# Moving the tiles of a matmul-bound kernel to start addresses that are multiples of 512 bytes

## Chip, cores and metric

The kernel runs on one core of one Trainium2 chip. The metric is the device time of one execution in microseconds (us), as the median of several runs. Durations of single instructions come from one profiled execution.

## What is computed

Three stages on 1536 tokens (2 batches of 768) with 512 features, all in float32:

```python
# 1. chunked attention, 8 heads of 64; a chunk of 32 queries sees 16 tokens left,
#    8 right, and 8 memory slots
scores = scale * np.matmul(q_c, k_full.transpose(0, 1, 3, 2))
a = np.exp(scores - np.max(scores, axis=-1, keepdims=True))
a = a / (np.sum(a, axis=-1, keepdims=True) + 1e-09)
out[:, :, c_start:c_end] = np.matmul(a, v_full)
# 2. a feed-forward layer 512 -> 2048 -> 512 with a rational function
h = x @ w_in;  h2 = h * h;  h3 = h2 * h
P = a[0] + a[1] * h + a[2] * h2 + a[3] * h3
Q = 1.0 + np.abs(b[0]) * np.abs(h) + np.abs(b[1]) * h2
x = (P / (Q + 1e-6)) @ w_out
# 3. four experts 512 -> 1024 -> 512, mixed with given shares
p = domain_probs / (domain_probs.sum(-1, keepdims=True) + 1e-09)
for e in range(4):
    h = np.maximum(x @ w1[e], 0.0)
    out += p[:, e:e + 1] * (h @ w2[e])
```

## The kernel before

**The large products.** Stages 2 and 3 multiply with TensorE. Each float32 operand is split into a high and a low half, both of type float32r, and each product is made of three matmuls (high with high, low with high, high with low; `PAIRS`). One such matmul has 128 x 128 stationary weights, a moving operand of 128 x 512 elements (2048 bytes in each partition) and one PSUM bank as its output. Each has a weight load of its own (512 bytes in each partition). There are 3366 of them:

- Stage 2 runs 48 steps (3 blocks of 512 tokens by 16 slices of 128 hidden features), each with 12 matmuls of `first_ops` (line 568: moving tile `x`, stationary tile `w`) and 12 of `second_ops` and `mm` (line 680: moving tile `g`, stationary tile `w`).
- Stage 3 runs 16 chunks of 256 hidden features. Chunk 0 has 72 matmuls at line 568 and 72 at line 927. Each of the chunks 1 to 15 has 42 matmuls at line 794 (seven products in Strassen's manner for two of the three blocks, stationary from `w`), 24 at line 568 (the third block) and 72 in `second` (line 927: moving tile `w`, stationary tile `g` or `gb`). Of the seven products at line 794, four move a tile `x`, and three move a sum of activations that lies in a tile `w`.

**The other engines.** VectorE (DVE), ScalarE (ACT) and GpSimd (POOL) split the weights and the activations, evaluate the rational function and read the PSUM banks out. All DMAs are issued by the SP queue.

**The order.** A planner (`Plan`) with costs and due times makes one list of operations; each engine gets its instructions in the order of that list. When the list is worked off, `make` allocates each tile at the operation that takes it first, and then the operation is recorded.

**Where tiles lie.** All tiles come from one pool. A tag gets its buffers side by side when it is taken for the first time, and the tags follow each other in that order, with no gap. In each partition 16,384 bytes of scratch and four constants of 32 bytes come first, then `ident` (512 bytes), `mask` (256), `cf` (64) and `pr` (192), which end at byte 17,536. Behind them lie, in the order of the list:

| tag | buffers x bytes | first byte | modulo 512 |
|---|---|---|---|
| `w` (weights, sums, attention's operands) | 10 x 8192 | 17,536 | 128 |
| `tm` | 2 x 2048 | 99,456 | 128 |
| `st` (row maxima and sums of attention) | 6 x 32 | 103,552 | 128 to 288 |
| `stg` (loaded weights) | 3 x 4096 | 103,744 | 320 |
| `x` (moving activations) | 12 x 4096 | 116,032 | 320 |
| `y`, `tu`, `ts` | 2, 2, 3 x 2048 | 165,184 | 320 |
| `g` | 4 x 4096 | 179,520 | 320 |
| `p` | 3 x 8192 | 195,904 | 320 |
| `gb` | 2 x 4096 | 220,480 | 320 |

Within these tiles every matmul at lines 568, 680, 794 and 927 begins at a multiple of 512 bytes, so that its operands begin at 128 modulo 512 if they lie in `w`, and at 320 modulo 512 if they lie in `x`, `g` or `gb`. `w` ends below byte 99,456; `x`, `g` and `gb` lie above byte 116,032.

The loop that allocates and records, lines 1102 to 1106:

```python
        for o in listed:
            for b in o.takes:
                make(b)
            o.fn()
            turn_over(fill.get(o, 0))
```

Of the kernel before, what the change touches and what calls it, by code (L numbers as in the profile page):

```python
# [11 lines left out]
F32 = mybir.dt.float32  # L12
# [33 lines left out]
AHEAD = 12  # L46
FU = 11
RU = 12
FGAP = 0.5
LAG = 3  # L50
GS = 4, 4, 4, 4
# [45 lines left out]
class Plan:  # L97
# [7 lines left out]
    def add(self, ways, fn, after=(), uses=(), takes=(), key=None, lock=False):  # L105
        op = Op(len(self.ops), ways, fn, key)
        op.lock = lock
        self.ops.append(op)
        for a in after:
            if a is not None:  # L110
                op.after.append(a)
                a.next.append(op)
        op.takes = list(takes)
        op.bufs = list(takes) + list(uses)
        for b in op.bufs:
            b.users.append(op)
        return op
# [133 lines left out]
def emit(ctx: ExitStack, tc: tile.TileContext, qk, v0, kv, q8, w64, w32, coef, prob, out):  # L251
# [8 lines left out]
    def sb(shape, dt, tag, name=None):  # L260
        return pool.tile(shape, dt, tag=tag, bufs=BUFS.get(tag, 1), name=name or tag)

    def bank(tag):
        return Buf(tag, [128, 512], F32)

    def make(b):
        p = psum if b.tag in ("acc", "h", "att") else pool
        b.ap = p.tile(b.shape, b.dt, tag=b.tag, bufs=BUFS[b.tag], name=b.tag)
# [22 lines left out]
    def turn_over(n):  # L291
        for _ in range(n):
            PE.matmul(idle.ap, zeros.ap[:, :128], zeros.ap, start=True, stop=True)
# [98 lines left out]
    class Unit:  # L392
# [5 lines left out]
        def psum_buf(self):  # L398
            if self.u >= RU:
                return bank("att")  # L400
            Unit.turn = (getattr(Unit, "turn", -1) + 1) % 6
            return bank((["att"] * 2 + ["acc"] * 4)[Unit.turn])
# [655 lines left out]
    o = add([("SP", 0.1)], load_probs, [steps[nA - 1].firsts[0]])  # L1058
# [30 lines left out]
    listed = plan.run()  # L1089
# [4 lines left out]
    for a, b in zip(pe, pe[1:]):  # L1094
        if a.n == last:
            break
        n = int((b.start - a.end - FGAP) / MM)
        if n > 0:
            fill[a] = min(n, 16)
    with tc.manual_schedule():  # L1100
        ACT.preload_act_table_set("natural_log_exp_and_others")
        for o in listed:
            for b in o.takes:
                make(b)
            o.fn()
            turn_over(fill.get(o, 0))

# [76 lines left out]
```

## Time and profile before

| | |
|---|---|
| median of 3 runs | 856.23 us (856.16 to 857.15) |
| the profiled execution | 855.45 us |
| its span, first to last instruction | 853.7 us |
| TensorE matmul busy | 835.5 us (98%) |
| DVE busy | 624.7 us (73%) |
| POOL busy | 380.6 us (45%) |
| ACT busy | 357.8 us (42%) |
| granted TensorE clock | 0.999 of full speed |

The profile lists instructions by line, engine and tile, each with its start. A matmul's own duration in it (some 390 ns) is the way of one matmul through a pipelined array: several overlap. What a matmul costs in a row of them is the distance from its start to the next one's start, so it is read from the starts of groups, or from the chain of work that ended last, which lists back-to-back stretches with their number of matmuls. The profile has no addresses; they are those of the table above.

### The profile page before, as it was taken

The page shows a single profiled execution, that of the slowest core. Times are in us where ns is not written, and L with a number is a line of the kernel's source. Part 1 is how long each engine was busy: PE and PEld are TensorE (multiplying, and loading weights), DVE is VectorE, ACT ScalarE, POOL GpSimd, SP SyncE. Part 2 cuts the span into 40 slices and gives each one's busy share as a digit, 9 for nine tenths or more (in the row PEclk, how much of TensorE's full clock was granted, in tenths as well). Part 3 has the DMA queues.
Part 4 walks back from the last instruction along what each step waited for, and adds up shares of the span by engine and source line. Part 5 has one row for each costly group of instructions (what it writes and reads, how often), then busy time and mean ns, then how long its engine had stood idle before and what let it go on. Part 6 is the DMA issues. An engine that isn't in the chain of part 4 may idle for free.

```text
span 853.7 us, 11342 instructions
## 1 busy us (share of the span) xinstructions
PE 835.5 (98%) x4214; PEld 665.2 (78%) x4218; DVE 624.7 (73%) x929; ACT 357.8 (42%) x783; POOL 380.6 (45%) x350
## 2 busy tenths in 40 slices
PE   7889999999999999999999999999999999999998
PEld 4667788778788887788888888888888888888886
DVE  6987799999996779775775775775765765765754
ACT  6798877756757665231231231231230230230210
POOL 4797776877678788440330330330330330330300
PEclk9999999999999999999999999999999999999999
DMA  9975122212212001010110110110110100100003
GB/s 350 362 263 194 51 74 74 90 60 74 74 49 52 1 0 50 1 51 0 50 40 10 50 38 12 49 32 18 50 30 20 50 28 22 50 25 1 1 1 147
DMA packets 21911, 55.41 MB, mean 65 GB/s; under 512 B 3936, under 2 KB 3936, under 8 KB 21856
## 3 DMA queue, kind: packets, MB, share of 16 engines
q1 hardware_dynamic: 21856, 54.69, 18.6%
q8 instruction: 33, 0.54, 0.3%
q14 instruction: 22, 0.18, 0.1%
HBM read 51.54 MB, written 3.15 MB: 64 GB/s over the span
## 4 chain that ended last, share of the span: by engine, by line
PE 66%; DVE 21%; ACT 4%; DMA 3%; POOL 3%; issue 2%; SPq 0%; DVEq 0%; ACTq 0%; POOLq 0%
PE acc L927 31%; PE att L568 11%; PE h L794 10%; PE att L794 7%; DVE ts L649 4%; PE h L568 3%; PE acc L680 3%; DVE tm L637 2%; DVE tm L641 2%; DVE p L699 2%; DVE y L357 2%; DVE y L363 1%; DVE y L351 1%; DVE att L649 1%; DMA w<-kv 1%
## 5 line engine op out<-in xcount | busy, mean ns | idle before, releaser
L325 POOL TENSOR_TENSOR w<-stg,w 128x512 fp32r<-128x512 f32 x64 | 97.0, 1525 | 325.4 <-ACT w L280 325.4
L944 DVE SCALAR_TENSOR_TENSOR p<-acc,pr,p 128x512 f32<-128x512 f32 x180 | 135.1, 751 | 107.1 <-PE acc L927 106.8
L927 PE MATMUL acc<-w,g 128*128 128x512 f32 x768 | 182.0, 397 | 0.5 <-DVE p L942 0.5
L927 PEld LDWEIGHTS acc<-w,g 128*128 128x128 f32 x768 | 144.9, 189 | 35.1 <-DVE p L942 1.4
L568 PE MATMUL att<-x,w 128*128 128x512 f32 x624 | 151.9, 395 | 1.5 <-DVE ts L649 1.5
L680 PE MATMUL acc<-g,w 128*128 128x512 f32 x576 | 146.3, 399 | 2.1 <-DVE p L699 1.6
L568 PEld LDWEIGHTS att<-x,w 128*128 128x128 f32 x624 | 116.9, 187 | 30.5 <-DVE ts L649 1.9
L680 PEld LDWEIGHTS acc<-g,w 128*128 128x128 f32 x576 | 106.9, 188 | 29.9 <-DVE p L699 3.0
L280 ACT ACTIVATE ts<-h 128x512 f32<-128x512 f32 x15 | 9.0, 599 | 246.0 <-PE h L794 246.0
L568 PE MATMUL h<-x,w 128*128 128x512 f32 x384 | 98.2, 400 | 0.5 <-DVE ts L649 0.3
L927 PE MATMUL acc<-w,gb 128*128 128x512 f32 x384 | 92.0, 397 | 0.0
L927 PEld LDWEIGHTS acc<-w,gb 128*128 128x128 f32 x384 | 72.6, 189 | 16.9
L568 PEld LDWEIGHTS h<-x,w 128*128 128x128 f32 x384 | 70.8, 188 | 17.7 <-POOL w L325 0.6
L325 POOL TENSOR_TENSOR g<-ts,g 128x512 fp32r<-128x512 f32 x48 | 66.7, 1391 | 26.8 <-ACT g L280 26.3
L668 POOL TENSOR_TENSOR ts<-ts,tu 128x512 f32<-128x512 f32 x48 | 63.3, 1320 | 12.9 <-ACT ts L657 9.6
L325 POOL TENSOR_TENSOR w<-y,w 128x512 fp32r<-128x512 f32 x36 | 49.9, 1387 | 8.3 <-ACT w L280 8.0
L280 ACT ACTIVATE g<-ts 128x512 fp32r<-128x512 f32 x48 | 30.3, 631 | 39.9 <-DVE ts L649 39.8
L794 PE MATMUL h<-x,w 128*128 128x512 f32 x180 | 46.8, 395 | 0.0
L794 PE MATMUL att<-x,w 128*128 128x512 f32 x180 | 46.8, 395 | 0.0
L794 PE MATMUL h<-w 128*128 128x512 f32 x180 | 46.0, 391 | 0.0
L794 PEld LDWEIGHTS h<-x,w 128*128 128x128 f32 x180 | 33.8, 188 | 8.2
L794 PEld LDWEIGHTS att<-x,w 128*128 128x128 f32 x180 | 33.8, 188 | 8.0
(122 smaller groups left out, 1167.8 us busy)
## 6 DMA issues: line engine op xcount, KB each, us to landing
stg<-w SPq DMA_DIRECT2D x64, 512.0 KB, 3.7
w<-kv SPq DMA_DIRECT2D x32, 256.0 KB, 5.9
w<-q SPq DMA_DIRECT2D x16, 256.0 KB, 5.8
w<-qk SPq DMA_DIRECT2D x8, 400.0 KB, 5.8
out<-p SPq DMA_DIRECT2D x12, 256.0 KB, 2.0
w<-v SPq DMA_DIRECT2D x8, 256.0 KB, 7.4
pr<-prob SPq DMA_DIRECT2D x1, 24.0 KB, 3.9
cf<-coef SPq DMA_DIRECT2D x1, 3.0 KB, 7.1
```

Source lines behind the costliest of these rows:

```text
L280: return lambda o, i: ACT.activation(o, i, AF.Copy)
L325: engines[op.eng].tensor_tensor(out=dst[:, 1], in0=src, in1=dst[:, 0].bitcast(F32), op=ALU.subtract)
L357: DVE.scalar_tensor_tensor(out=y.ap, in0=words(1), scalar=-(1 << 30), in1=y.ap, op0=ALU.bitwise_and, op1=ALU.bitwise_or,)
L568: PE.matmul(s.h.ap, wt[w].ap[:, 0, a, k * 128 : (k + 1) * 128], xs[k].ap[:, b], start=(k == 0 and n == 0), stop=(k == KT - 1 and n == 2),)
L637: [("DVE", 0.6)], lambda: DVE.tensor_tensor(out=m.ap, in0=m.ap, in1=h.ap, op=ALU.mult), [li], [h, m]
L641: lambda: DVE.scalar_tensor_tensor(out=m.ap, in0=m.ap, scalar=A1, in1=h.ap, op0=ALU.add, op1=ALU.mult),
L649: lambda: DVE.scalar_tensor_tensor(out=out.ap, in0=in0.ap, scalar=scalar, in1=in1.ap, op0=op0, op1=op1),
L668: lambda: POOL.tensor_tensor(out=s.ap, in0=s.ap, in1=u.ap, op=ALU.mult), [ln], [s, u],
L680: PE.matmul(ps, wt[f].ap[:, 1, a, d * 128 : (d + 1) * 128], g.ap[:, b], start=start, stop=stop)
L794: PE.matmul(ps.ap, left(a, k), right(b, k), start=k == 0 and n == 0, stop=k == 1 and n == 2,)
L927: PE.matmul(ps.ap, gs[j][0].ap[:, a, d * 128 : d * 128 + 128], wt[f].ap[:, 1, b], start=j == 0 and n == 0, stop=j == 1 and n == 2,)
L944: DVE.scalar_tensor_tensor(out=y, in0=ps.ap, scalar=p, in1=y, op0=ALU.mult, op1=ALU.add)
```

## The change

Ahead of the loop the buffers of tag `st` are now allocated, and behind them a tile `pad` of 192 bytes that nothing reads or writes. The loop leaves out the one buffer that has been made already.

```diff
+PAD = 192 // 4
 ...
     with tc.manual_schedule():
         ACT.preload_act_table_set("natural_log_exp_and_others")
+
+        make(next(b for o in listed for b in o.takes if b.tag == "st"))
+        sb([128, PAD], F32, "pad")
         for o in listed:
             for b in o.takes:
-                make(b)
+                if b.ap is None:
+                    make(b)
             o.fn()
             turn_over(fill.get(o, 0))
```

So `st` starts at byte 17,536 and `pad` at 17,728, and `w` starts at 17,920, which is 35 x 512. `w` and `tm` move up by 384 bytes, every later tag by 192 bytes, and all tags from `w` on start at 0 modulo 512. `gb` ends at byte 228,864. Every engine has the same instructions in the same order, with the same waits; only addresses in SBUF differ. No instruction is added, removed or moved.

## Rows read from the trace of the kernel before

**Rows 1.** Page, busy time by engine; then windows: busy us and instructions of each engine.

```profile
PE 835.5 (98%) x4214; PEld 665.2 (78%) x4218; DVE 624.7 (73%) x929; ACT 357.8 (42%) x783; POOL 380.6 (45%) x350
...
core 0: us, PE busy (x) PEld busy (x) DVE busy (x) ACT busy (x) POOL busy (x), PEclk, DMA share, GB/s
110.00:250.00 140.00, 138.11 (x586) 109.59 (x586) 132.91 (x186) 96.24 (x163) 105.73 (x81) 1.00 0.21 72
250.00:320.00 70.00, 70.00 (x302) 56.43 (x300) 50.09 (x74) 45.60 (x78) 53.50 (x46) 1.00 0.07 16
362.00:835.00 473.00, 473.00 (x2035) 382.78 (x2034) 307.68 (x424) 107.61 (x190) 112.66 (x85) 1.00 0.09 28
```

**Rows 2.** Waits of PE in the whole span: engine, line, releaser, us, times, longest.

```profile
PE acc L680 <- DVE p L699: 1.6, 2, 0.9
PE att L568 <- DVE ts L649: 1.5, 1, 1.5
```

**Rows 3.** Chain that ended last, 496 to 529 us: start us, us, what.

```profile
496.56 1.40 PE h L794 x6
497.96 1.40 PE att L794 x6
499.36 1.38 PE h L794 x6
500.74 1.38 PE att L794 x6
502.12 1.36 PE h L794 x6
503.48 1.40 PE att L794 x6
504.88 1.40 PE h L794 x6
506.28 5.60 PE att L568 x24
511.88 16.80 PE acc L927 x72
528.68 1.40 PE h L794 x6
```

**Rows 4.** Timeline of PE, 499 to 506 us: which tiles those products read.

```profile
499.19 1.54 PE L794 MATMUL h<-w 128*128 128x512 f32 x6
501.96 1.52 PE L794 MATMUL h<-w 128*128 128x512 f32 x6
503.32 1.56 PE L794 MATMUL att<-x,w 128*128 128x512 f32 x6
506.12 5.76 PE L568 MATMUL att<-x,w 128*128 128x512 f32 x24
```

**Rows 5.** Timeline of PE near 36 us, and line 293: bfloat16 matmuls on zeros.

```profile
36.57 1.24 PE L293 MATMUL acc<-tm 128*128 128x512 bf16 x5 [0.16 <-issue]
...
L293 PE MATMUL acc<-tm x16: 379/384/634, 1.2 to 48.0; 128*128 128x512 bf16 x16
```

**Rows 6.** Waits of DVE, 110 to 250 us.

```profile
DVE y L351 <- POOL w L325: 2.4, 2, 1.2
DVE ts L649 <- ACT h L672: 1.6, 3, 0.9
```

**Rows 7.** Chain that ended last, 100 to 345 us (stage 2): pieces on PE and one on DVE.

```profile
105.55 4.67 PE acc L680 x20
113.72 2.81 PE h L568 x12
120.71 1.25 DVE y L363
```

**Rows 8.** Groups by line and shape: VectorE reading tile tm (128) and tile ts (320).

```profile
L637 DVE TENSOR_TENSOR tm<-tm,h 128x512 f32<-128x512 f32 x29 | 19.7, 678 | 1.9 <-ACT tm L634 1.8
L649 DVE SCALAR_TENSOR_TENSOR ts<-ts,h 128x512 f32<-128x512 f32 x29 | 19.7, 678 | 0.2
```

## The prediction

> **What bounds the kernel now.** I read the busy times first, then the waits of PE, then the chain of work that ended last. PE is busy for 835.5 of 853.7 us [rows 1], and the two longest sums of waits that the list of PE's waits has are 1.6 and 1.5 us [rows 2]. So PE works almost throughout, and the question is what one matmul costs there. The granted clock is 1.00 in every stretch [rows 1], that is 2.4 GHz, at which 512 columns take 512 / 2.4 = 213.3 ns. The chain shows whole stretches in which each matmul follows the one before: 24 at line 568 take 5.60 us and 72 at line 927 take 16.80 us, both 233.3 ns each [rows 3]; stage 2 has the same, 20 at line 680 in 4.67 us and 12 at line 568 in 2.81 us, 233.5 and 234 ns [rows 7]. Each costs 20 ns more than its columns.
>
> Not every matmul does. The reader should look at the seven pieces of line 794 in one chunk: four of 1.40 us, two of 1.38 us and one of 1.36 us, for six matmuls each [rows 3]. The shape, the weight loads, the number of matmuls per PSUM bank and the halves used are the same in all seven. The timeline tells what differs: the short ones read only `w` ("h<-w"), the long ones read `x` and `w` [rows 4]. By the table of addresses both operands of the short ones begin at 128 modulo 512; in the long ones the moving operand begins at 320 and the stationary one at 128. At line 927 it is the other way round, moving `w` at 128 and stationary `g` or `gb` at 320, and it costs 233.3 ns as well. So in the trace of the kernel before there are two classes: both operands at 128, 226.7 ns (1.36 / 6) to 230 ns (1.38 / 6); one of them at 320, 233.3 ns. The difference is up to 6.7 ns, and the change puts all of them into one class.
>
> There is a third row, of another type: five bfloat16 matmuls on a zero tile at 128 modulo 512 are busy for 1.24 us together, and one of them lasts 0.384 us by the median [rows 5], so four distances make 0.86 us, 215 ns each, 1.7 ns over 512 columns. It is the nearest row for a matmul without the extra time.
>
> **The change part by part.** *Added work:* none. `pad` is never read or written, no engine gets an instruction, and `make` runs when the program is built, not on the chip. *Bytes:* all transfers and all operands are as large as before. *PSUM:* no address moves.
>
> *VectorE, ScalarE, GpSimd.* Their operands move too. The profile has VectorE reading the tile `tm` (at 128) and the tile `ts` (at 320), each with one PSUM operand, at 678 ns in both [rows 8]. I take their prices as unchanged. For what lies at neither of the two offsets there is no row; the bounds are nothing on either side, because stage 3 would hide some per cent on an engine that is busy for 307.68 of 473 us [rows 1], and stage 2 would not. If VectorE changed by 1% there, it would be some 1.3 of 132.91 us either way, and I leave that to the range.
>
> *The matmuls.* The new offsets are 0 and 0 everywhere. Like 128 and 128 they are equal, and like 128, 0 is a multiple of 128 bytes, which 320 is not. No row has an fp32r operand at 0, so the price is bounded. From above it is 233.3 + 6.7 = 240 ns (one more step of the size seen, see the rivals); from below it is the 215 ns of the bfloat16 row. I take the row nearest in type, shape and kind of address, the pieces that read only `w`: 1.38 us per six for the first two products of a chunk and 1.36 us from then on, as now.
>
> Sum against the profiled execution (855.45 us), stretch by stretch:
>
> 1. Chunks 1 to 15. Now the seven products take 4 x 1.40 + 2 x 1.38 + 1.36 = 9.72 us; then 2 x 1.38 + 5 x 1.36 = 9.56 us. Line 568 goes from 5.60 to 24 x 0.2267 = 5.44 us, line 927 from 16.80 to 16.32 us. That is 0.16 + 0.16 + 0.48 = 0.80 us a chunk of 32.12 us (496.56 to 528.68 us [rows 3]), and 12.0 us in 15. Nothing else is late there: DVE is busy for 307.68 and POOL for 112.66 of 473 us [rows 1], and the chain runs on PE alone [rows 3].
> 2. Chunk 0: 144 matmuls x 6.7 ns = 0.96 us at most. PE waits there for 1.5 us for DVE in one place [rows 2]; I take 0.7 us.
> 3. The last part of stage 2, 250 to 320 us: PE is busy for all 70.00 us with 302 matmuls, DVE for 50.09 and POOL for 53.50 [rows 1]. 302 x 6.7 ns = 2.0 us, all of it.
> 4. The middle of stage 2, 110 to 250 us: 586 matmuls, 3.9 us at most. But DVE is busy for 132.91 of these 140 us, with 2.4 us of waits for POOL and 1.6 us for ACT in its row of waits [rows 1, 6], and the chain passes through DVE [rows 7]. A faster PE here mostly waits for DVE's rational function and its conversions. I take a third, 1.3 us.
> 5. The rest of stage 2 (48 x 24 = 1152 in all, less 302 and 586: some 260 matmuls, in groups between the attention's small ones and at the change of stages): 1.7 us at most. The first 26 us have no large product and stay. I take 0.5 us.
>
> The sum is 12.0 + 0.7 + 2.0 + 1.3 + 0.5 = 16.5 us, so the profiled execution would be 838.95 us. The median of the runs is 0.78 us above the profiled execution; from the median it is 856.2 - 16.5 = 839.7 us. If all of 1 to 5 came, it would be 12.0 + 0.96 + 2.0 + 3.9 + 1.7 = 20.6 us, 835.6 us. If every matmul stayed at 230 ns, as in the first two products, half of it would come, some 8 us: 848 us. These are this forecast's own ends.
>
> **The rivals.** *The extra time goes altogether.* The 13.3 ns that are left at 128 and 128 (226.7 - 213.3) may themselves come from the start. For it: 128 bytes are 32 columns of 4 bytes, which take 13.3 ns, and from 320 to the next multiple of 256 it is 192 bytes, 48 columns, 20.0 ns. That is just the extra time of the two classes, as if the way to the next multiple of 256 were paid. Against it: the same 20 ns come where only the weights lie at 320, so that it would have to be the worse of two ways rather than their sum, and the bfloat16 row at 128 pays hardly any of it. At 215 ns a chunk saves 120 x 18.3 + 18 x 13.9 ns = 2.45 us (228.9 ns is the mean of the three pieces on `w`), 36.7 us in 15; chunk 0 saves 2.0, stretch 3 some 4.5 (POOL's 53.50 us would then stand against 65), stretches 4 and 5 some 3 as DVE holds them. That is 46 us: 810 us.
>
> *Nothing changes.* What separates the classes may be where tiles lie rather than at which offset they start: the short ones have both operands below byte 99,456, the others have one above 116,032, and the change keeps that. The trace can't tell the two, as every tile above starts at 320. Also for it: the same two tiles ("h<-w") cost 230 or 226.7 ns in one chunk, at one offset, so something else than the offset has a hand in it. Then the time stays 856.2 us. Against it: nothing in the trace suggests that one reading of 512 columns is slower by its place. The Trainium skill (TensorE: Matmul & The Clock Gate, section "Wait — 56ns, not 53.3ns?") speaks for this rival: it gives the distance of warm matmuls by the columns alone, 215.7 ns at 512, with no term for an address, and its page SBUF — State Buffer (section "Operand start alignment") calls the start address a matter of legality, not speed. By that rule the sum would be nothing; the bfloat16 row agrees with it, and the two classes of float32r rows, both above 215.7 ns, do not.
>
> *Slower.* While a matmul streams, the weights of the next are read. If the two readings disturb each other when both begin at the start of the same 512-byte stretch, the step of 6.7 ns would be added to 233.3 instead of being taken away: 240 ns. The path is PE alone, so it would count in full: 3096 x 6.7 ns + 270 x 11 ns = 24 us, 880 us. It decides as soon as a matmul at 0 and 0 costs more than 233.3 ns. Against it: the fastest rows today are those with equal offsets.
>
> **How the numbers follow.** The forecast, 839.7 us, has 0.47; all of the extra time gone, 810 us, 0.25; no change, 856.2 us, 0.20; slower, 880 us, 0.08. A range that leaves out at most 2 in 10 can do without the slower case alone, as 0.08 + 0.20 or 0.08 + 0.25 is already too much; it runs from the floor case to no change with a little for the spread of the runs, 809 to 858 us. Faster and slower are told apart at 0.2% (1.7 us), about what a measurement of this kernel can tell. From the four cases: faster 0.47 + 0.25 = 0.72, same 0.19, slower 0.09, with 0.01 of the third case beyond the bound.
>
> **What would show it.** In the chain of the changed kernel, line 927's 72 matmuls should take 16.3 us, line 568's 24 should take 5.44 us, and the seven products at line 794 should take the same time each whether they read `x` or not. 16.80 us again would mean that the place and not the offset makes the classes; 15.5 us would be the rival in which all of it goes. In stage 2 PE's waits for DVE at lines 649 and 699 should grow between 110 and 250 us, and hardly elsewhere. VectorE's 678 ns should stay. The prediction is wrong if matmuls cost the same as before, or if PE gains in stage 3 and loses it to waits that are not there now.

## The result and the profile after

The changed kernel takes 843.36 us as the median (843.05 to 844.18) beside 856.19 us for the kernel before (855.07 to 857.15): ratio 0.9851, 95% interval 0.9837 to 0.9865. It is 12.8 us faster; 16.5 us were forecast. The profiled execution took 843.32 us.

The chain of work that ended last, in the same chunk as [rows 3] (start us, us, what; lines are one higher than before):

```profile
493.71 1.36 PE h L795 x6
495.07 1.36 PE att L795 x6
496.43 1.36 PE h L795 x6
497.79 1.36 PE att L795 x6
499.15 1.36 PE h L795 x6
500.51 1.36 PE att L795 x6
501.87 1.36 PE h L795 x6
503.23 5.44 PE att L569 x24
508.67 16.32 PE acc L928 x72
524.99 1.36 PE h L795 x6
```

All seven products take 1.36 us, and so do the others in proportion: 5.44 / 24 and 16.32 / 72 are 226.7 ns. The class of 233.3 ns is gone. A chunk takes 524.99 - 493.71 = 31.28 us instead of 32.12.

Up to there next to nothing has come of it. The same piece, the third block's products in chunk 1, begins at the same time in both executions, as their chains show, of the kernel before:

```profile
378.12 5.60 PE att L568 x24
```

and of the changed kernel:

```profile
378.11 5.44 PE att L569 x24
```

Counted from the first large matmul of stage 2, which starts at 26.79 us in the one and at 27.32 us in the other, it comes 0.5 us earlier in the changed kernel.

Stage 2 says how. The windows (busy us and instructions of PE, PEld, DVE, ACT, POOL), of the kernel before from 110 to 345 us:

```profile
110.00:345.00 235.00, 231.60 (x986) 184.49 (x986) 207.58 (x292) 154.94 (x262) 178.27 (x141) 1.00 0.16 52
```

and of the changed kernel, with the two parts that answer to [rows 1] and the waits of PE from 110 to 345 us (engine, line, releaser: us, times, longest):

```profile
110.00:345.00 235.00, 228.96 (x986) 185.17 (x984) 206.72 (x293) 154.74 (x261) 178.98 (x141) 0.99 0.16 52
...
110.00:250.00 140.00, 136.08 (x581) 109.51 (x580) 132.59 (x187) 95.90 (x161) 105.94 (x81) 0.99 0.21 72
250.00:320.00 70.00, 70.00 (x310) 57.87 (x310) 49.55 (x73) 45.97 (x78) 53.48 (x47) 1.00 0.06 16
...
PE acc L681 <- DVE p L700: 3.0, 3, 2.1
PE att L569 <- DVE ts L650: 1.7, 1, 1.7
```

PE starts 986 matmuls in these 235 us in both kernels. It is busy for 2.64 us less and waits longer for DVE: 3.0 us for the read-outs at line 700 instead of the 1.6 us of [rows 2]. The chain at the longest of these waits runs on DVE alone, of the changed kernel:

```profile
228.43 0.75 DVE ts L650
229.17 0.67 DVE h L650
229.84 2.38 DVE p L700 x4
```

In the kernel before the same four read-outs are a piece of the same length:

```profile
229.27 2.38 DVE p L699 x4
```

DVE reaches them no earlier with a faster PE: here 0.57 us later, in an execution whose large matmuls began 0.53 us later. They stand behind DVE's own queue, and PE's next matmuls at line 681 need the banks that they free.

The two parts by themselves, 581 matmuls instead of 586 up to 250 us and 310 instead of 302 from there on, mislead, because the granted clock fell in this execution behind that wait. A window of it, and the 12 matmuls that follow the wait:

```profile
232.00:234.00 2.00, 2.00 (x5) 1.43 (x5) 2.00 (x5) 1.15 (x3) 0.56 (x2) 0.50 0.03 8
...
230.58 5.34 PE L681 MATMUL acc<-g,w 128*128 128x512 f32 x12 [2.07 <-DVE p L700]
```

The clock of 0.50 is the level of 1.2 GHz; from 236 us it is 1.00 again. The 12 matmuls take 235.76 - 230.58 = 5.18 us. One kernel of the next section (everything at 128) has the same instructions and matmuls as fast, and its clock stayed at 1.00 here:

```profile
110.00:250.00 140.00, 135.88 (x587) 109.47 (x586) 132.01 (x186) 95.89 (x162) 106.55 (x81) 1.00 0.22 72
250.00:320.00 70.00, 69.31 (x303) 56.30 (x301) 50.06 (x74) 45.63 (x78) 53.54 (x47) 1.00 0.06 16
...
229.26 2.38 DVE p L700 x4
...
229.99 4.03 PE L681 MATMUL acc<-g,w 128*128 128x512 f32 x12 [2.09 <-DVE p L700]
```

Its large matmuls begin at 26.69 us, and DVE's read-outs start within 0.01 us of where they start in the kernel before. The 12 matmuls take 3.88 us (to 233.87) behind a wait as long, and the two parts have 587 and 303 matmuls, one more in each than before. So DVE's pace leaves PE next to nothing in either part; the 310 of the changed kernel only made up for what the low clock had cost (581 + 310 = 891 matmuls, here 587 + 303 = 890). The piece in chunk 1 begins at 377.63 us there, 0.4 us earlier by the count from the first large matmul.

### The profile page after: what moved, and what is told of

The parts are those of the page before. It is cut to its first block, busy times and chain, and to the rows that moved or that the text cites. A ratio compares the mean times of both kernels' runs of the same rounds, so it can differ in the third digit from the quotient of the medians.

```text
span 841.5 us, 11342 instructions
## 1 busy us (share of the span) xinstructions
PE 819.9 (97%) x4214; PEld 664.9 (79%) x4218; DVE 623.6 (74%) x929; ACT 356.5 (42%) x783; POOL 381.1 (45%) x350
## 4 chain that ended last, share of the span: by engine, by line
PE 65%; DVE 21%; ACT 5%; POOL 4%; issue 2%; DMA 2%; SPq 0%; DVEq 0%; ACTq 0%; POOLq 0%
PE acc L928 30%; PE att L569 10%; PE h L795 10%; PE att L795 7%; DVE ts L650 5%; PE h L569 3%; PE acc L681 3%; DVE tm L638 2%; DVE tm L642 2%; DVE p L700 2%; DVE y L358 2%; DVE y L352 1%; DVE att L650 1%; DVE y L364 1%; DMA w<-kv 1%
## 5 line engine op out<-in xcount | busy, mean ns | idle before, releaser
L928 PE MATMUL acc<-w,g 128*128 128x512 f32 x768 | 177.5, 390 | 0.7 <-DVE p L943 0.6
L569 PE MATMUL att<-x,w 128*128 128x512 f32 x624 | 147.8, 390 | 1.7 <-DVE ts L650 1.7
L569 PE MATMUL h<-x,w 128*128 128x512 f32 x384 | 96.5, 396 | 1.0 <-DVE ts L650 0.8
L928 PE MATMUL acc<-w,gb 128*128 128x512 f32 x384 | 89.6, 389 | 0.0
L669 POOL TENSOR_TENSOR ts<-ts,tu 128x512 f32<-128x512 f32 x48 | 63.8, 1329 | 12.8 <-ACT ts L658 10.9
L795 PE MATMUL h<-x,w 128*128 128x512 f32 x180 | 45.7, 389 | 0.0
L795 PE MATMUL att<-x,w 128*128 128x512 f32 x180 | 45.7, 389 | 0.0
```

What stands on the lines that cost most here:

```text
L569: PE.matmul(s.h.ap, wt[w].ap[:, 0, a, k * 128 : (k + 1) * 128], xs[k].ap[:, b], start=(k == 0 and n == 0), stop=(k == KT - 1 and n == 2),)
L669: lambda: POOL.tensor_tensor(out=s.ap, in0=s.ap, in1=u.ap, op=ALU.mult), [ln], [s, u],
L795: PE.matmul(ps.ap, left(a, k), right(b, k), start=k == 0 and n == 0, stop=k == 1 and n == 2,)
L928: PE.matmul(ps.ap, gs[j][0].ap[:, a, d * 128 : d * 128 + 128], wt[f].ap[:, 1, b], start=j == 0 and n == 0, stop=j == 1 and n == 2,)
```

## Which property of the addresses counts

The change made the starts multiples of 512 bytes, and with that also multiples of 128, and equal to each other. The forecast named the last two together. Six kernels take them apart. In all of them the instructions are the same, and each tag lies within a few hundred bytes of where the changed kernel has it, or the kernel before.

**Everything at 320.** The changed kernel without its rest of 192 bytes:

```diff
         make(next(b for o in listed for b in o.takes if b.tag == "st"))
-        sb([128, PAD], F32, "pad")
```

> The small buffers are moved ahead, but the 192 bytes are left out, so that every tile from w on begins at 320 modulo 512: both operands of each large product begin at equal offsets, and neither is a multiple of 128 bytes. Theory of equal offsets: 226.7 ns a matmul everywhere, a chunk takes 31.28 us as after the change, and the time is that of the changed kernel, 843 us. Theory of multiples of 128 bytes: both operands are off, so 233.3 ns or more everywhere, a chunk takes at least 32.2 us (the three products on w get slower too), and the time is 857 us or above. Theory of place: as after the change, 843 us.

Measured: 843.5 us, ratio 0.9854 (0.9840 to 0.9869). The chain:

```profile
496.58 1.36 PE att L795 x6
504.74 5.44 PE att L569 x24
510.18 16.32 PE acc L928 x72
```

No large operand begins at a multiple of 512 here, nor of 128, and a matmul costs 226.7 ns all the same. The rest of 192 bytes does nothing; moving `st` ahead is the whole effect. Before, its six buffers of 32 bytes stood between `tm` and `stg` and put 192 bytes between the offset of `w` and that of `x`, `g` and `gb`. The half of my reason on multiples of 128 falls. So does the rival of place: `x`, `g` and `gb` lie at the very bytes of the kernel before, and `w` 192 bytes higher.

**Everything at 128.**

```diff
-PAD = 192 // 4
+PAD = 320 // 4
```

> 320 bytes instead of 192, so that every tile from w on begins at 128 modulo 512. Equal offsets and multiples of 128 bytes both say 226.7 ns everywhere and 843 us. If only multiples of 512 count, line 928 takes more than 16.32 us for 72 matmuls: up to 230 ns each (16.56 us), as the products on w did before the change, a chunk up to 31.7 us, and 849 us.

Measured: 843.37 us, ratio 0.9848 (0.9834 to 0.9863), with 1.36, 5.44 and 16.32 us in the chain. The same 128 and 128 had cost 230 ns in two of the three products on `w` before [rows 3]. So those 230 ns were no price of the offset 128, but an after-effect of the slower matmuls ahead of them.

**Different starts, all multiples of 128.** Rests between the tags: `w` at 0, `x` at 128, `g` at 256, `gb` at 384.

```diff
+PADS = {'x': 128, 'g': 128, 'gb': 128}
 ...
             for b in o.takes:
+                if b.tag in PADS:
+                    sb([128, PADS.pop(b.tag) // 4], F32, "pad_" + b.tag)
```

> The changed kernel with more rests between the tags: w stays at 0 modulo 512, x begins at 128, g at 256, gb at 384. All are multiples of 128 bytes, and the two operands of a product begin at different offsets except for the three products on w. Theory of equal offsets: 233.3 ns at lines 569, 681, 928 and for the products that read x, 226.7 ns for the three on w, 856 us. Theory of multiples of 128 bytes: 226.7 ns everywhere, 843 us. Theory of multiples of 512: above 226.7 ns wherever x, g or gb is read, and not the same for 128, 256 and 384.

Measured: 850.84 us, ratio 0.9935 (0.9920 to 0.9950), between both forecasts. The timeline of PE (start us, busy us) shows a mixture, in stage 2 and in stage 3:

```profile
265.90 2.90 PE L682 MATMUL acc<-g,w 128*128 128x512 f32 x12
268.63 2.95 PE L570 MATMUL att<-x,w 128*128 128x512 f32 x12
271.42 2.90 PE L682 MATMUL acc<-g,w 128*128 128x512 f32 x12
...
510.31 11.06 PE L929 MATMUL acc<-w,g 128*128 128x512 f32 x48
521.21 5.75 PE L929 MATMUL acc<-w,gb 128*128 128x512 f32 x24
526.80 1.56 PE L796 MATMUL h<-x,w 128*128 128x512 f32 x6
```

From start to start: `g` at 256 moving past `w` at 0 takes 2.73 / 12 = 227.5 ns, `w` moving past `g` at 256 takes 10.90 / 48 = 227.1 ns; but `x` at 128 takes 2.79 / 12 = 232.5 ns and `gb` at 384 takes 5.59 / 24 = 232.9 ns. A difference of 256 bytes is as good as none; one of 128 or 384 is not. None of the three theories had said that.

**Smaller differences.** The same edit with 32 bytes three times: `x` at 32, `g` at 64, `gb` at 96.

> As the mixed kernel, but with smaller rests: w at 0 modulo 512, x at 32, g at 64, gb at 96. One run shows the moving operand off by 32 (lines 569 and 795) and by 64 (line 681), and the stationary one off by 64 and 96 (line 928). Theory of multiples of 128 bytes: 233.3 ns at 64 in either role, as at 320 before, and at least that at 32 and 96, so 856 us or above. Equal offsets say the same of this run. If 64-byte starts are enough when the offset of the other is 0, 226.7 ns at 64.

Measured: 856.11 us, ratio 1.0001 (0.9992 to 1.0011): with differences of 32 to 96 bytes the whole gain is gone, though `w` begins at a multiple of 512. The timeline:

```profile
266.61 2.91 PE L682 MATMUL acc<-g,w 128*128 128x512 f32 x12
269.36 2.96 PE L570 MATMUL att<-x,w 128*128 128x512 f32 x12
272.15 2.91 PE L682 MATMUL acc<-g,w 128*128 128x512 f32 x12
...
480.38 11.36 PE L929 MATMUL acc<-w,g 128*128 128x512 f32 x48
491.58 5.77 PE L929 MATMUL acc<-w,gb 128*128 128x512 f32 x24
497.19 1.56 PE L796 MATMUL h<-x,w 128*128 128x512 f32 x6
```

`g` at 64 costs 11.20 / 48 = 233.3 ns as the stationary operand, but 2.75 / 12 = 229.2 ns as the moving one; `x` at 32 costs 2.79 / 12 = 232.5 ns and `gb` at 96 costs 5.61 / 24 = 233.8 ns.

**The rule tried on the kernel before.** If only the difference modulo 256 counts, 64 bytes more behind `st`, where it stood, must do: `w` stays at 128, and the others go to 384.

```diff
+    rest = [64 // 4]
 ...
             for b in o.takes:
                 make(b)
+                if b.tag == "st" and rest:
+                    sb([128, rest.pop()], F32, "pad")
```

> The kernel before, with one edit: a rest of 64 bytes behind st, where st stands. w and tm stay at 128 modulo 512; x, g and gb go from 320 to 384, so that the two operands of every large product differ by 256 bytes, or not at all. Theory that only the difference modulo 256 counts: 226.7 ns everywhere, a chunk 31.28 us, 843 us. Theory that the operands have to begin at equal places modulo 512 or at multiples of 512: 233 ns or about that wherever x, g or gb is read, 856 us.

Measured: 843.76 us, ratio 0.9852 (0.9837 to 0.9867). The chain:

```profile
502.58 5.44 PE att L568 x24
508.02 16.32 PE acc L927 x72
```

Every product of stages 2 and 3 then has operands that differ by 256 bytes or not at all, in either role, and all cost 226.7 ns. No operand of a large product begins at a multiple of 256.

**Other differences.** `w` at 0, `x` at 64, `g` at 192, `gb` at 224 (one execution).

> The changed kernel with w at 0 modulo 512, x at 64, g at 192, gb at 224: differences that are no multiple of 256 in both roles. Theory of the difference modulo 256: between 229 and 234 ns at lines 570, 682 and 929, 226.7 to 228 ns for the three products on w, 850 to 856 us. It also tells whether the 229 ns that line 682 showed with g at 64 belong to that difference: then x at 64 gives 229 ns too, at lines 570 and 796, and 853 us; or to that line, then 233 ns and 856 us.

Measured: 851.78 us. The timeline:

```profile
263.26 2.91 PE L570 MATMUL h<-x,w 128*128 128x512 f32 x12
266.01 2.95 PE L682 MATMUL acc<-g,w 128*128 128x512 f32 x12
268.80 2.91 PE L570 MATMUL att<-x,w 128*128 128x512 f32 x12
...
480.24 11.16 PE L929 MATMUL acc<-w,g 128*128 128x512 f32 x48
491.24 5.75 PE L929 MATMUL acc<-w,gb 128*128 128x512 f32 x24
496.83 1.55 PE L796 MATMUL h<-x,w 128*128 128x512 f32 x6
```

`x` at 64 takes 2.75 / 12 = 229.2 ns, so that price belongs to the difference and not to line 682; `g` at 192 takes 2.79 / 12 = 232.5 ns moving and 11.00 / 48 = 229.2 ns stationary, `gb` at 224 takes 5.59 / 24 = 232.9 ns. So a difference that is no multiple of 256 costs 229 to 234 ns. Where the moving operand lies 64 bytes above the other modulo 256, these two kernels show 229.2 ns in each of the three cases; but line 927 of the kernel before (128 and 320) is the same difference, and it takes 233.3 ns. What sets the price among the unequal ones stays open, and so does whether a matmul is slowed by its own weight load or by the next one's: neighbours in these rows have the same starts.

## Where stage 2's share went

Theory: DVE sets the pace of stage 2 at its read-outs and at its end, and a faster PE only waits there. Rival: the matmuls of stage 2 gain nothing, or something else holds its length. To tell them apart, DVE gets less to do, with the old addresses and with the new, and the gain from the addresses is compared.

**Without the third conversion of each stage-2 weight.** The edit is the same in both kernels; the last three mantissa bits of those weights are left out.

```diff
-            o = add([("DVE", 0.6)], conv3, [o], [r, y], lock=True)
+            o = add([("DVE", 0.6)], lambda: None, [o], [r, y], lock=True)
```

> The kernel before (old addresses) without the third conversion of each stage-2 weight (line 363 there, 32 instructions, 28.3 us of DVE in all, most of it in stage 2): the last three mantissa bits of those weights are left out, nothing else. It is the base for the next run. If DVE sets the pace of stage 2, stage 3 begins earlier than at 362 us by some us; if PE does, by nearly nothing.

> The changed kernel (all tiles at 0 modulo 512) without the same conversion. Theory that DVE took back what PE gained in stage 2: with DVE relieved, stage 2 now gains from the addresses, so that stage 3 begins 3 to 6 us earlier than in the run with the old addresses and the same conversion left out, and the whole is 15.5 to 18.5 us faster than that run, against 12.9 us with the conversion. Rival, that large products of stage 2 gain nothing from the addresses themselves or that another wait (ACT, POOL) holds stage 2: stage 3 begins at the same time in both, and the whole differs by 12 to 13 us.

Measured: 851.30 us with the old addresses and 838.54 us with the new ones. The difference is 12.8 us, as with the full work, and the piece of chunk 1 begins at 374.01 and 374.00 us. The large matmuls began 1.2 us later with the new addresses (28.60 instead of 27.37 us; the granted clock was 0.87 instead of 0.93 in the first 26 us), so that stage 2 itself may have kept 1.2 us. The 3 to 6 us of the theory did not come: its expectation failed. The waits of PE with the new addresses, from 110 to 345 us:

```profile
PE att L569 <- DVE ts L650: 1.7, 1, 1.7
PE acc L681 <- DVE p L700: 1.5, 2, 0.8
```

Old addresses leave one wait of 0.4 us in this list. So PE still waits for DVE, now longest near 327 us. The last weight conversion begins at 240 us, so the relief does not reach the place where DVE is late. Whether that is the reason was tried with a relief that reaches to the end.

**Less in every step.** In addition to the conversion one of the multiplications of the rational function is left out in all 48 steps, which changes the output.

```diff
-                [("DVE", 0.6)], lambda: DVE.tensor_tensor(out=m.ap, in0=m.ap, in1=h.ap, op=ALU.mult), [li], [h, m]
+                [("DVE", 0.6)], lambda: None, [li], [h, m]
```

> The kernel before (old addresses) without the third weight conversion (last three mantissa bits of the stage-2 weights) and without one of the multiplications of the rational function (line 637: m times h, 48 instructions of 0.68 us), so that the output of stage 2 is another one; some 58 us less on DVE. It is the base of the next run. If DVE holds stage 2, its end comes earlier than in the run without the conversion alone, which began chunk 1 some 4 us earlier than the kernel before.

> The changed kernel with the same two things left out. Theory that DVE takes back in stage 2 what PE gains: with DVE relieved through all 48 steps and up to their end, stage 2 keeps 3 to 6 us of its gain, and the run is 16 to 19 us faster than the one with the old addresses. Rival, that something else holds stage 2's length (start of the run, DMA, ACT, POOL): the difference stays at 12 to 13 us, as with the full work (12.9) and without the conversion (12.8).

Measured: 849.18 us with the old addresses, 830.80 us with the new: 18.4 us apart. The windows, old addresses and then new:

```profile
110.00:345.00 235.00, 234.88 (x1007) 189.12 (x1007) 177.07 (x243) 159.33 (x269) 182.90 (x146) 1.00 0.16 52
```

```profile
110.00:345.00 235.00, 234.08 (x1030) 192.89 (x1029) 180.53 (x248) 159.49 (x270) 184.98 (x147) 1.00 0.16 51
```

PE now starts 1030 matmuls instead of 1007, 2.3% more, where it had been 986 in both; its waits for DVE in this stretch are 0.9 us. The large matmuls began at 27.46 and 27.43 us, and the piece of chunk 1 begins 6.2 us earlier, old addresses and then new:

```profile
371.87 5.60 PE att L568 x24
...
365.70 5.44 PE att L569 x24
```

So stage 2 and chunk 0 gain 6.2 us by the addresses, of 8.7 us at most (1152 and 144 matmuls x 6.7 ns), once DVE is relieved; with its full work DVE took nearly all of it back. This relief is both larger than the one before and reaches further; which of the two was needed is not told apart.

**The planner told of the new cost.** The changed kernel with one number:

```diff
-MM = 0.2325
+MM = 0.2267
```

> The changed kernel with the planner's cost of one large matmul set from 0.2325 to 0.2267 us, which is what it now takes. The order of the work on the other engines follows the due times, so DVE's late read-outs in stage 2 may come earlier relative to PE. If the two waits of some 2 and 1 us for DVE in stage 2 come from the order alone, 1 to 3 us faster than the changed kernel, 840 to 842 us; if from DVE's load, the same 843 us within 1 us; a worse order could cost 1 to 2 us.

Measured: 841.85 us (839.96 to 842.10), ratio to the kernel before 0.9825 (0.9807 to 0.9843). Its median is 1.5 us below that of the changed kernel, inside the 1 to 3 us that an order to blame would give, but the two ratios' intervals overlap, so it is not told apart from the changed kernel. PE's longest wait for DVE in stage 2 only moves, from line 700 to line 650:

```profile
PE h L569 <- DVE ts L650: 3.1, 2, 2.2
```

## The prediction, step by step

- **What bounds the kernel, and the two classes.** Right: 226.7 ns is what every large matmul costs after the change, with no 230 ns left.
- **Chunks 1 to 15.** Forecast 0.80 us a chunk and 12.0 us; measured 0.84 us a chunk, because the two products on `w` that were kept at 1.38 us went to 1.36 us as well. From the piece at 378 us to the end of the span it is 853.7 - 378.12 = 475.6 us before and 841.5 - 378.11 = 463.4 us after, 12.2 us. The two spans differ by as much, 853.7 - 841.5 us.
- **Chunk 0 and stage 2.** Forecast 0.7 + 2.0 + 1.3 + 0.5 = 4.5 us; measured 0.5 us up to the piece in chunk 1, some 0.2 us of it from chunk 1's own seven products, and 0.4 us with everything at 128 (counted alike: 0.4 us at 320, 1.0 us with 64 bytes more behind `st`). These are the terms of the sum that were mis-sized. From 250 to 320 us I booked 2.0 us, "all of it", because PE was busy throughout and DVE for 50.09 of 70 us only. With everything at 128 PE got through 303 matmuls there instead of 302 and waited 0.6 us for DVE's read-outs, where it had waited for nothing before. From 110 to 250 us I took a third where the row said that DVE was busy for 132.91 of 140 us: it was one matmul, 587 instead of 586. A stretch in which PE never waits was not PE's own here: with faster matmuls PE ran into DVE's read-outs there too.
- **The reason.** "Equal" was right, "a multiple of 128 bytes" was not: 320 and 320 does as well (0.9854), 128 and 0 does not (232.5 ns). The two could not be told apart in the trace of the kernel before, and I should have given them a chance each.
- **All of the extra time gone.** It is not: 13.3 ns over 512 columns remain at equal offsets, at 0 as at 128 and 320. The arithmetic with the way to the next multiple of 256 was a coincidence; 256 does count, but as the modulus of the difference.
- **Nothing changes.** The place in SBUF plays no part: at 320 and 320 the tiles `x`, `g` and `gb` lie where they did, and the time is 843.5 us. The Trainium skill (TensorE: Matmul & The Clock Gate, "Wait — 56ns, not 53.3ns?") has the distance of warm matmuls by their columns alone, and its page SBUF — State Buffer ("Who interferes with whom") has two independent read ports for PE. Here the same 512 columns take 226.7 or 233.3 ns by the difference between the starts of the operands of those two readings, so for float32r operands the columns alone do not give the distance, and the two readings are not independent of each other in time.
- **Slower.** Equal starts do not disturb each other; they are the fastest.
- **VectorE.** The groups of [rows 8] take 680 ns each after the change instead of 678, which is as good as unchanged.

## What to carry to other kernels

Where the chain is PE alone, as in stage 3 here, the addresses of the operands can be worth time without any change of an instruction: read the distance of matmul starts by pairs of tiles, and where two pairs of the same shape differ, look at where both operands begin, the moving against the stationary one. Small odd-sized buffers belong ahead of or behind all large tiles, so that they do not shift some of them against others. And before a gain per matmul is multiplied by the number of matmuls, find the stages that another engine paces: here that stage gave 0.5 us of the 4.5 forecast, and 6.2 us only when that engine had less to do. DVE's busy share of the stretch that I had booked whole, 50.09 of 70 us, did not show it.

## What was not expected of the hardware

- A float32r matmul of 512 columns with its own weight load takes 226.7 ns where moving and stationary operand begin at the same place modulo 256 bytes, wherever that is (0, 128 or 320 in both; 0 and 256; 128 and 384), and 229 to 234 ns at the differences tried that are no multiple of 256 (32, 64, 96, 128, 192, 224).
- The slower matmuls have an after-effect: in the kernel before, products with equal starts ran at 230 ns for 12 matmuls behind unequal ones and then at 226.7 [rows 3]; where all are equal (0, 128 or 320 in both), each of the seven products takes 1.36 us in every chunk, and none ran at 230 ns.
- The granted clock fell to 0.50 behind a wait of PE of 2.07 us in the changed kernel's execution, and stayed at 1.00 behind one of 2.09 us with everything at 128; what decides that is open. Twelve matmuls took 5.18 us instead of 3.88 us by it, and yet the piece in chunk 1 came no later, counted from the first large matmul (350.8 and 350.9 us): DVE set the pace there.
